# A causal convolution and a ReGLU feed-forward layer on one core: the second unit's convolution in 64x64 matmuls, a shared first Relu, another order of lanes and evictions

## The chip, the cores and the metric

The kernel runs on one core of a Trainium2 chip. The core has a matrix engine (TensorE, PE in the profile, with PEld for its weight loads), VectorE (DVE), ScalarE (ACT), GpSimd (POOL), and SyncE (SP), whose queue here does nothing but issue DMAs. Each engine works through its own list of instructions in order; they wait for each other through semaphores. The metric is the device time of one execution in microseconds.

## The reference

`x` is (8, 4096, 192). A causal convolution of 7 taps, with one set of softmax weights for each of 8 heads of 24 channels, goes into a feed-forward layer with 1536 hidden columns:

```python
w = softmax(weight, axis=-1)                    # (8 heads, 7 taps)
x_pad = concatenate([zeros((B, 6, D)), x], 1)
conv[b, s, h, g] = sum_k w[h, k] * x_pad[b, s + k, h, g]
x = conv.reshape(32768, 192)
out = (maximum(x @ w_gate, 0) * (x @ w_val)) @ w_out
```

Inputs and output are float32; the kernel computes in float16 with float32 accumulation.

## The kernel before

**Units.** The eight sequences are taken as four pairs, `st` = 0 and 1, and each pair is cut into units of 1024 tokens: 16 units. Of each unit the kernel needs `xc`, the convolved tokens turned so that channels lie on partitions: 64 channels of sequence 0 on partitions 0 to 63, the same 64 of sequence 1 on 64 to 127, for 3 groups of channels. Then `gate_val` computes the hidden layer for two windows of 512 tokens, and `project` computes the output for both.

**gate_val.** For each of 12 slices `f` of the hidden layer PE fills two PSUM tiles of 2 x 512 columns, one for the gate and one for the value (`L505`, 12 matmuls each of 64 rows; two of them, for the two sequences, lie in the upper and lower half of the array). ScalarE takes the Relu of the gate tile into `gr` (`L514`), and VectorE multiplies it with the value tile into `hT` (`L515`). There are four PSUM tiles (`psum`, 4 buffers, all named `ps`), so a slice waits for the Relu and the product of the slice two before it.

**project.** Unit 0 uses matmuls over the full array (`half_whole`, `L555`), 48 for each of four half windows; later units use half arrays (`L535`). ScalarE copies the outputs out of PSUM (`L572`) and SP writes them.

**Three ways to convolve.** Unit 0 (groups of tokens 0 and 1) is convolved by PE with x as weights and a band matrix as moving data (`conv_dense`, `L333`), already turned. Units 2 to 15 are convolved by the "lanes" on VectorE, ScalarE and GpSimd, two units ahead: `lane_load` loads, `lane_turn` copies on GpSimd (`L433`) and turns by nine DMA transposes on SP (`L436`), `lane_first` is the first tap on ScalarE (`L469`), `lane_rest` the other taps on VectorE (`L481`, `L454`), and products by ScalarE (`L452`, in `project`) are added on GpSimd (`add`, `L458`).

**The second unit** is what the change rewrites. Its 1024 tokens are cut into sub-blocks of 112 (`SUB`), the last one overlapping, in two groups of five (groups 2 and 3). `load_x` puts the 118 tokens that a sub-block needs on 118 partitions, with both sequences side by side. `conv(g, part)` multiplies by the band of a head (118 x 112) as weights: four heads of a group in each of two calls, one matmul of 240 columns per head (5 sub-blocks, 2 sequences, 24 channels), `L358`. `PLACE` says which bank and slot a head gets. Five copies on ScalarE (`move`, `L373`) put the result into `y` in the order of channels that the turn needs, and five DMA transposes on SP (`L395`) turn `y` straight into `xc[1]`, 112 tokens each.

**Order.** The schedule is by hand (`manual_schedule`): each engine gets its instructions in the order of the Python text. In unit 0: `gate_val(0, 0)`, `lane_turn(2)`, `load_x(3)`, `gate_val(0, 1)`, `conv(2, 0)`, `conv(2, 1)`, `lane_first(2)`, `lane_rest(2)`, then `project`, in which `conv(3, 0)` and `conv(3, 1)` follow the first of four half windows. Unit 1 begins with an `add`, `lane_load(3)` and two more `add` on GpSimd.

The tile pools give a new tile the buffer of an old one of the same name; `epool` has one buffer each for `x_e` and `x_p`, the tiles of `lane_load` and `lane_turn`.

Of the kernel before, what the change touches and what calls it, by code (L numbers as in the profile page):

```python
# [9 lines left out]
F16 = mybir.dt.float16  # L10
# [5 lines left out]
def kernel(  # L16
# [58 lines left out]
    def load_x(g):  # L75


        bp, toks = GROUPS[g]
        xt = xpool.tile([128, GSUB, 2, D], F16, name="x_h")
        rows, step = (SUB, DSUB) if g < 2 else (128, SUB)  # L80
        for st in range(2):
            b = bp + NB * st
            last = toks[-1] - toks[-2] != step
            n_full = len(toks) - int(last)
            src = bass.AP(
                tensor=x.tensor,
                offset=x.offset + (b * S + toks[0] - PAD) * D,
                ap=[[D, rows], [step * D, n_full], [1, D]],
            )
            nc.gpsimd.dma_start(out=xt[0:rows, 0:n_full, st, :], in_=src)  # L90
            if last:
                nc.gpsimd.dma_start(
                    out=xt[0 : SUB + PAD, len(toks) - 1, st, :],
                    in_=x[b, toks[-1] - PAD : toks[-1] + SUB, :],
                )
        return xt

    xts = {}
# [181 lines left out]
    bands = {}  # L280

    def fill_band(a, heads, copy):
        lo, n = heads[0] - HB * a, len(heads)
        part = const.tile([128, n, SUB], F16, name=f"band{heads[0]}")
        for i, h in enumerate(heads):
# [16 lines left out]

    PLACE = {0: (0, 0, 0), 1: (0, 0, 1), 3: (0, 1, 0), 4: (0, 1, 1)}
    PLACE |= {6: (1, 0, 0), 7: (1, 0, 1), 2: (1, 1, 0), 5: (1, 1, 1)}

    def conv_dense(g, c):

# [32 lines left out]
        copy = nc.vector.tensor_copy if c == 1 else nc.scalar.copy  # L342
        copy(out=xc[0][:, c, t0 : t0 + WIN], in_=ps[:, 0, :])

    convs = {}

    def conv(g, part):


        xt = xts[g]  # L350
        bp, toks = GROUPS[g]
        n = len(toks)
        rows = SUB + PAD
        W = 2 * n * G
        ps = psum.tile([128, 2, 512], FP, name="ps")
        for h, (t, bank, slot) in PLACE.items():
            if t == part:
                nc.tensor.matmul(  # L358
                    out=ps[0:SUB, bank, W * slot : W * (slot + 1)],
                    lhsT=band(h),  # L360
                    rhs=xt[0:rows, 0:n, :, G * h : G * (h + 1)],
                    start=True,
                    stop=True,
                    skip_group_check=True,
                )
        if part == 0:
            convs[g] = ypool.tile([128, GSUB, NCH, 2, 64], F16, name="y")
        y = convs[g]

        def move(copy, bank, i0, step_in, c, r0, step_out, width):  # L370
            src = ps[0:SUB, bank, 0 : 2 * W]
            dst = y[0:SUB, 0:n, 0, :, 0:1]
            copy(  # L373
                out=bass.AP(
                    tensor=dst.tensor,
                    offset=dst.offset + 128 * c + r0,
                    ap=[dst.ap[0], [step_out, 2], [NCH * 128, n], [64, 2], [1, width]],
                ),
                in_=bass.AP(
                    tensor=src.tensor,  # L380
                    offset=src.offset + i0,
                    ap=[src.ap[0], [W + step_in, 2], [2 * G, n], [G, 2], [1, width]],
                ),
            )

        if part == 0:
            move(nc.scalar.copy, 0, 0, 0, 0, 0, G, G)
            move(nc.scalar.copy, 1, 0, 0, 1, 8, G, G)
            return
        move(nc.scalar.copy, 0, 0, 0, 2, 16, G, G)  # L390
        move(nc.scalar.copy, 1, 0, 8, 0, 48, 2 * 128 - 48, 16)
        move(nc.scalar.copy, 1, 16, -16, 1, 0, 56, 8)
        for jj, t in enumerate(toks):
            u, k = t // UNIT, min(SUB, UNIT - t % UNIT)
            nc.sync.dma_start_transpose(  # L395
                out=xc[u][:, :, t % UNIT : t % UNIT + k],
                in_=y[0:k, jj].rearrange("p c s r -> p (c s r)"),
            )

    xes, xrs, accs, prods = {}, {}, {}, {}  # L400

# [90 lines left out]
    def gate_val(u, w):  # L492
        h = hpool.tile([128, NFF, 2, WIN], F16, name="hT")
        xcb = xc[u]
        for f in range(NFF):
            if u == 0 and w == 0 and f in (5, 7, 9):
                conv_dense(1, (f - 5) // 2)
            pss = [psum.tile([128, 2, 512], FP, name="ps") for _ in range(2)]
            order = [(i, c) for i in range(2) for c in range(NCH)]
            if u == 0 and w == 0 and f == 0:  # L500
                order = [(i, c) for c in range(NCH) for i in range(2)]
            for i, c in order:
                W = (Wg, Wv)[i]
                for st in range(2):
                    nc.tensor.matmul(  # L505
                        out=pss[i][:, st, :],
                        lhsT=W[64 * st : 64 * st + 64, c, 128 * f : 128 * (f + 1)],
                        rhs=xcb[64 * st : 64 * st + 64, c, WIN * w : WIN * (w + 1)],
                        start=(c == 0),
                        stop=(c == NCH - 1),  # L510
                        tile_position=(64 * st, 0),
                    )
            gr = gpool.tile([128, 2, WIN], F16, name="gr")
            nc.scalar.activation(out=gr[:], in_=pss[0][:], func=ACTF.Relu)  # L514
            nc.vector.tensor_tensor(out=h[:, f], in0=gr[:], in1=pss[1][:], op=ALU.mult)  # L515
        return h

# [75 lines left out]
    def project(u, hs, work):  # L593
        bp, w0 = u * UNIT // S, u * UNIT % S // WIN
        at, done = {}, {}
        order = [(0, 0), (1, 0), (0, 1), (2, 0), (1, 1), (3, 0), (2, 1), (3, 1)]
        if u == 0:
            order = [(i, 2) for i in range(4)]
        if u == NUNIT - 1:
            order = [(0, 0), (1, 0), (0, 1), (2, 0), (1, 1), (2, 3), (3, 0), (2, 4), (3, 1)]  # L600
        for i, turn in order:
            final = u == NUNIT - 1 and i == 3
            h, st = hs[i // 2], i % 2
            if turn in (0, 2):
                at[i] = slots(final)
            if turn in (1, 2):
                for c, k in work[i]:
                    product(nc.scalar, u + 2, c, k)
            if turn > 2:
                n = turn - 3  # L610
                half_pass(h, st, at[i][1], final, 1, done.pop(i, None), (n,))
                put(
                    nc.scalar.copy,
                    nc.sync,
                    at[i][0][0][:, :, D * n : D * n + D],
                    (bp + NB * st) * S + WIN * (w0 + i // 2) + 128 * n,
                    2,
                    256,
                )
                continue  # L620
            if turn == 2:
                half_whole(h, st, at[i][1])
            else:
                done[i] = half_pass(h, st, at[i][1], final, turn, done.get(i))
            if turn:
                evict(at[i][0], (bp + NB * st) * S + WIN * (w0 + i // 2), final, u > 0 and i == 3)
            if u == 0 and i == 0:
                conv(3, 0)
                conv(3, 1)


    for c in range(NCH):
# [9 lines left out]
    for u in range(NUNIT):  # L642
# [2 lines left out]
            add(u + 1, 1)  # L645
        if u == 1:
            lane_load(3)
            add(2, 2)
            add(2, 3)
        hs = []  # L650
# [3 lines left out]
            lane_turn(u + 2)  # L654
        if u == 0:
            xts[3] = load_x(3)
        if 0 < u < NUNIT - 3:
            lane_load(u + 3)
        if lane:
# [5 lines left out]
            add(u + 1, KW - 1)  # L665
        if u == 0:
            xc[1] = xcpool.tile([128, NCH, UNIT], F16, name="xc")
            conv(2, 0)
            conv(2, 1)
        del xc[u]  # L670
        work = [[] for _ in range(4)]
        if u + 2 < NUNIT:
            lane_first(u + 2)
            lane_rest(u + 2)
            todo = [(c, k) for k in (0, 1, 2, 3, 4, 6) for c in range(NCH)]
            todo = [ck for ck in todo if ck not in VECTOR[u > 0]]
            cut = [0, 4, 8, 12, 16] if u == 0 else [0, 5, 10, 15, 16]
            work = [todo[a:b] for a, b in zip(cut, cut[1:])]
# [31 lines left out]
```

## Time and profile before

| what | value |
|---|---|
| runs | 769.03, 769.03, 769.93 us; median 769.03 us |
| the profiled execution, its time | 768.24 us |
| its span, first to last instruction | 766.5 us |
| granted TensorE clock, mean | 1.00 |
| chain of waits, share of the span by engine | PE 98%, DMA 1%, all else under 1% |

The profile is of one execution. Busy times count instructions, not waits; L numbers are lines of the kernel above. A row of the groups of instructions is: line, engine, operation, output and inputs with sizes, count, then busy time in us and the mean of one in ns, then idle time of the engine just before. The convolutions on PE and what belongs to the second unit's are small rows among large ones:

```profile
L505 PE MATMUL ps<-xc,Wv 64*128 64x512 f16 x2304 | 311.8, 376 | 0.2 <-DVE hT L515 0.2
L535 PE MATMUL ps<-Wo,hT 64*128 64x192 f16 x5760 | 240.1, 243 | 0.0
L358 PE MATMUL ps<-x_h,band 118*112 118x240 f16 x16 | 2.0, 268 | 0.0
L358 PEld LDWEIGHTS <-band 118*112 118x112 f16 x16 | 1.6, 129 | 0.4 <-issue 0.4
```

The mean of one PE instruction (376 ns) is longer than the distance between two of them, since they are pipelined: a unit's 288 matmuls of L505 stand 31.08 us in the chain, 0.108 us each. The queue of SP from 20 us on, in order of time:

```profile
30.66 13.19 SPq L436 DMA_TRANSPOSE x_r<-x_p  x9
...
50.93 0.53 SPq L573 DMA_DIRECT2D out_dram<-out_s  x1
51.57 8.51 SPq L395 DMA_TRANSPOSE xc<-y  x5
60.19 1.86 SPq L573 DMA_DIRECT2D out_dram<-out_s  x3
76.30 12.53 SPq L436 DMA_TRANSPOSE x_r<-x_p  x9
```

and GpSimd's, which is idle from 33 us to 60.73 us:

```profile
60.73 3.02 POOL L458 TENSOR_TENSOR prods<-prods 128x1344 f32<-128x1344 f32 x1 [27.56 <-DVE prods L454]
63.71 3.27 POOL L414 DMA_DIRECT2D x_e<-in_x_dram  x4
66.97 6.17 POOL L458 TENSOR_TENSOR prods<-prods 128x1344 f32<-128x1344 f32 x2
73.08 3.19 POOL L433 COPY x_p<-x_e 128x1728 f16<-128x1728 f16 x2
```

### The profile page before, as it was taken

To read this page: it belongs to the slowest core of one execution; us is meant where nothing else is said; L and a number is where in the kernel's file an instruction comes from. 1 tells how busy PE (TensorE), PEld (TensorE's weight loads), DVE (VectorE), ACT (ScalarE), POOL (GpSimd) and SP (SyncE) were. 2 spreads that over 40 slices of the span, in tenths; PEclk is the share of its full clock that TensorE was granted. 3 is DMA by queue.
4 is the path that set the end of the run, shared out by engine and by line. 5 is a ranking of instruction groups with operands and counts; after the bars stand their busy time and mean duration, and the time that the engine had idled before them with its cause. 6 is when DMAs were issued, how large, how long until landed. Compare 5 with 4: busy or idle time off the path is not lost.

```text
span 766.5 us, 24874 instructions
## 1 busy us (share of the span) xinstructions
PE 761.7 (99%) x10842; PEld 502.6 (66%) x10842; DVE 691.8 (90%) x743; ACT 601.1 (78%) x734; POOL 369.8 (48%) x212
## 2 busy tenths in 40 slices
PE   9999999999999999999999999999999999999998
PEld 4495674946749476584765848567494674947648
DVE  6999999999999999999999999999999999996590
ACT  6797887878878787887878878788787887874571
POOL 8608638093470935619166290743908346090000
PEclk9999999999999999999999999999999999999999
DMA  8956727180372804528054271722819131200202
GB/s 121 138 101 114 92 89 89 50 126 6 99 79 64 112 22 93 66 86 94 23 110 48 85 92 44 108 29 85 93 44 114 24 94 38 65 22 18 68 2 84
DMA packets 131826, 56.12 MB, mean 73 GB/s; under 512 B 96757, under 2 KB 131717, under 8 KB 131717
## 3 DMA queue, kind: packets, MB, share of 16 engines
q1 hardware_dynamic: 90805, 38.85, 24.8%
q0 software_dynamic: 40768, 15.59, 18.5%
q8 instruction: 84, 1.38, 0.8%
q14 instruction: 25, 0.20, 0.1%
q10 hardware_dynamic: 144, 0.10, 0.0%
HBM read 31.68 MB, written 25.17 MB: 74 GB/s over the span
## 4 chain that ended last, share of the span: by engine, by line
PE 98%; DMA 1%; DVE 0%; ACT 0%; issue 0%; POOL 0%; POOLq 0%
PE ps L505 65%; PE ps L535 31%; PE ps L555 2%; DMA x_h<-in_x_dram 1%; PE ps L333 0%; PE ps L358 0%; DVE hT L515 0%; ACT gr L514 0%; DVE acc L572 0%; POOL spaced L129 0%; POOLq L694 0%
## 5 line engine op out<-in xcount | busy, mean ns | idle before, releaser
L515 DVE TENSOR_TENSOR hT<-gr,ps 128x1024 f16<-128x1024 f16 x384 | 468.7, 1221 | 37.6 <-ACT gr L514 10.7
L514 ACT ACTIVATE gr<-ps 128x1024 f16<-128x1024 f32 x384 | 392.8, 1023 | 102.8 <-PE ps L505 101.1
L458 POOL TENSOR_TENSOR prods<-prods 128x1344 f32<-128x1344 f32 x70 | 212.4, 3034 | 309.6 <-DVE prods L454 306.2
L505 PE MATMUL ps<-xc,Wv 64*128 64x512 f16 x2304 | 311.8, 376 | 0.2 <-DVE hT L515 0.2
L505 PE MATMUL ps<-xc,Wg 64*128 64x512 f16 x2304 | 311.9, 376 | 0.0
L535 PEld LDWEIGHTS <-hT 64*128 64x128 f16 x5760 | 238.0, 94 | 3.6
L535 PE MATMUL ps<-Wo,hT 64*128 64x192 f16 x5760 | 240.1, 243 | 0.0
L505 PEld LDWEIGHTS <-Wv 64*128 64x128 f16 x2304 | 129.9, 94 | 118.8 <-issue 0.5
L505 PEld LDWEIGHTS <-Wg 64*128 64x128 f16 x2304 | 112.2, 94 | 132.4 <-issue 0.2
L481 DVE SCALAR_TENSOR_TENSOR acc<-x_r,tap,acc 128x576 f32<-128x576 f16 x210 | 154.3, 811 | 1.6 <-DMA x_r<-x_p 1.6
L452 ACT ACTIVATE prods<-x_r,tap 128x448 f32<-128x448 f16 x222 | 130.3, 662 | 0.0
L572 ACT COPY out_s<-ps 128x768 f32<-128x768 f32 (+1 forms) x64 | 46.1, 721 | 54.0 <-PE ps L535 44.0
L414 POOL DMA_DIRECT2D x_e<-in_x_dram x56 | 45.2, 819 | 3.3 <-POOL x_p L433 3.3
L433 POOL COPY x_p<-x_e 128x1728 f16<-128x1728 f16 x28 | 44.7, 1622 | 2.0 <-DMA x_e<-in_x_dram 2.0
L458 POOL TENSOR_TENSOR xc<-prods 128x1344 f16<-128x1344 f32 x14 | 42.4, 3026 | 1.1
L481 DVE SCALAR_TENSOR_TENSOR xc<-x_r,tap,acc 128x576 f16<-128x576 f16 x42 | 31.8, 810 | 0.0
L469 ACT ACTIVATE acc<-x_r,tap 128x576 f32<-128x576 f16 x42 | 29.4, 766 | 0.0
L454 DVE TENSOR_SCALAR prods<-x_r,tap 128x448 f32<-128x448 f16 x72 | 27.3, 445 | 0.0
L572 DVE COPY out_s<-ps 128x384 f32<-128x384 f32 x14 | 7.7, 549 | 14.8 <-ACT out_s L572 14.8
L555 PE MATMUL ps<-Wo,hT 128*128 128x192 f16 x192 | 16.2, 246 | 0.0
L555 PEld LDWEIGHTS <-hT 128*128 128x128 f16 x192 | 15.9, 98 | 0.0
L572 DVE COPY acc<-ps 128x192 f32<-128x192 f32 x1 | 0.4, 357 | 14.2 <-PE ps L535 14.2
(52 smaller groups left out, 63.2 us busy)
## 6 DMA issues: line engine op xcount, KB each, us to landing
out_dram<-out_s SPq DMA_DIRECT2D x62, 384.0 KB
x_e<-in_x_dram POOLq DMA_DIRECT2D x34, 192.0 KB, 6.2
x_e<-in_x_dram POOLq DMA_DIRECT2D x22, 240.0 KB, 4.6
x_r<-x_p SPq DMA_TRANSPOSE x126
Wo<-in_moe_w_out_dram POOLq DMA_DIRECT2D x1, 576.0 KB, 10.2
x_h<-in_x_dram POOLq DMA_DIRECT2D x2, 240.0 KB, 7.8
x_h<-in_x_dram POOLq DMA_DIRECT2D x2, 210.0 KB, 5.2
x_h<-in_x_dram POOLq DMA_DIRECT2D x2, 192.0 KB, 7.5
```

The lines of the kernel that those rows point to most:

```text
L414: nc.gpsimd.dma_start(out=xe[:, j : j + n, st, :, :].rearrange("p j c r -> p j (c r)"), in_=bass.AP(tensor=x.tensor, offset=x.offset + (b ...
L433: nc.gpsimd.tensor_copy(out=xp[:, :, :, st, :], in_=xe[:, :, st, :, :])
L452: engine.activation(out=out, in_=in_, func=ACTF.Copy, scale=scale)
L458: nc.gpsimd.tensor_tensor(out=pr[:, 0] if k < KW - 1 else xc[u][:, :, LDVE:UNIT], in0=pr[:, 0], in1=pr[:, k], op=ALU.add,)
L469: nc.scalar.activation(out=accs[u][:, c, :], in_=shifted(u, c, 0, 0), func=ACTF.Copy, scale=tap[:, c, 0:1],)
L481: nc.vector.scalar_tensor_tensor(out=xc[u][:, c, 0:LDVE] if k == KW - 1 else acc[:, c, :], in0=shifted(u, c, k, 0), scalar=tap[:, c, k : k ...
L505: nc.tensor.matmul(out=pss[i][:, st, :], lhsT=W[64 * st : 64 * st + 64, c, 128 * f : 128 * (f + 1)], rhs=xcb[64 * st : 64 * st + 64, c, WI ...
L514: nc.scalar.activation(out=gr[:], in_=pss[0][:], func=ACTF.Relu)
L515: nc.vector.tensor_tensor(out=h[:, f], in0=gr[:], in1=pss[1][:], op=ALU.mult)
L535: mm = nc.tensor.matmul(out=outs[q], lhsT=h[64 * r : 64 * r + 64, f, st, 128 * q : 128 * (q + 1)], rhs=Wo[64 * r : 64 * r + 64, f, :], sta ...
L555: nc.tensor.matmul(out=outs[q], lhsT=h[:, f, st, 128 * q : 128 * (q + 1)], rhs=Wo[:, f, :], start=(f == 0), stop=(f == NFF - 1),)
L572: one(out=dst[:, step * j : step * j + step], in_=src[:, step * j : step * j + step])
```

## The change

Four edits.

1. **64x64 matmuls.** For groups 2 and 3 `load_x` puts sequence 0 on partitions 0 to 63 and sequence 1 on 64 to 127, and cuts each sub-block into two windows of 64 tokens that give 56 outputs each (`HALF`). `conv` runs, for each head, four matmuls of 120 columns, one for each sequence and window, each in its own quarter of the array (`tile_position`). The weights are the upper left 64 x 64 of the band; for the lower quarters they are read from `lower`, a copy on partitions 64 to 127 that three GpSimd copies make (`fill_lower`, behind `load_x(3)`). The five copies into `y` now cover 128 partitions, and the two sequences come from two PSUM banks.
2. **Gaps closed on GpSimd.** Each window leaves 8 rows that are no output. The five SP transposes of a group now turn all 128 rows of `y` into a tile `turned` (in the buffer of `x_e` for group 2, of `x_p` for group 3), and `close_up` copies 56 of every 64 columns into `xc[1]`: one copy for group 2, two for group 3. `close_up(2)` stands behind `conv(3, 1)`, `close_up(3)` in unit 1 behind `lane_load(3)`.
3. **The first Relu shared.** In the first slice of the first window VectorE takes the Relu of one half of the gate tile (a maximum with 0), ScalarE of the other.
4. **Lanes first.** `conv(2, 0)` and `conv(2, 1)` are called after `lane_first(2)` and `lane_rest(2)`.

```diff
+            n_full = len(toks) - int(toks[-1] - toks[-2] != SUB)
+            for j, n in ((0, n_full), (n_full, len(toks) - n_full)):
+                if n:
+                    nc.gpsimd.dma_start(
+                        out=xt[64 * st : 64 * st + 64, j : j + n].rearrange("p n w d -> p (n w) d"),
+                        in_=bass.AP(
+                            tensor=x.tensor,
+                            offset=x.offset + (b * S + toks[j] - PAD) * D,
+                            ap=[[D, 64], [SUB // 2 * D, 2 * n], [1, D]],
+                        ),
+                    )
...
+    PLACE = [(0, 1, 3, 4), (6, 7, 2, 5)]
+    HALF = SUB // 2
+    lower = const.tile([128, H, 64], F16)
+
+    def fill_lower():
+        for h0, n in ((0, 3), (3, 1), (4, 4)):
+            nc.gpsimd.tensor_copy(out=lower[64:128, h0 : h0 + n], in_=parts[h0][0:64, :, 0:64])
...
-        for h, (t, bank, slot) in PLACE.items():
-            if t == part:
-                nc.tensor.matmul(
-                    out=ps[0:SUB, bank, W * slot : W * (slot + 1)],
-                    lhsT=band(h),
-                    rhs=xt[0:rows, 0:n, :, G * h : G * (h + 1)],
...
+        for slot, h in enumerate(PLACE[part]):
+            for w in range(2):
+                for st in range(2):
+                    nc.tensor.matmul(
+                        out=ps[64 * w : 64 * w + 64, st, W * slot : W * (slot + 1)],
+                        lhsT=lower[64:128, h] if st else band(h)[0:64, 0:64],
+                        rhs=xt[64 * st : 64 * st + 64, 0:n, w, G * h : G * (h + 1)],
...
+                        tile_position=(64 * st, 64 * w),
...
-        for jj, t in enumerate(toks):
-            u, k = t // UNIT, min(SUB, UNIT - t % UNIT)
             nc.sync.dma_start_transpose(
-                out=xc[u][:, :, t % UNIT : t % UNIT + k],
-                in_=y[0:k, jj].rearrange("p c s r -> p (c s r)"),
-            )
+                out=turned[:, :, jj].rearrange("p c w s -> p c (w s)"),
+                in_=y[:, jj].rearrange("p c s r -> p (c s r)"),
+            )
+        turns[g] = turned
+
+    def close_up(g):
+        turned, toks = turns.pop(g), GROUPS[g][1]
+        n = len(toks)
+        n_full = n - int(toks[-1] - toks[-2] != SUB)
+        for j, m in ((0, n_full), (n_full, n - n_full)):
+            t = toks[j % n] % UNIT
+            if m:
+                nc.gpsimd.tensor_copy(
+                    out=xc[1][:, :, t : t + SUB * m].rearrange("p c (n s) -> p c n s", s=HALF),
+                    in_=turned[:, :, j : j + m, :, 0:HALF].rearrange("p c n w s -> p c (n w) s"),
+                )
...
-            nc.scalar.activation(out=gr[:], in_=pss[0][:], func=ACTF.Relu)
+            own = int(u == 0 and w == 0 and f == 0)
+            if own:
+                nc.vector.tensor_scalar(
+                    out=gr[:, 0], in0=pss[0][:, 0], scalar1=0.0, scalar2=None, op0=ALU.max
+                )
+            nc.scalar.activation(out=gr[:, own:2], in_=pss[0][:, own:2], func=ACTF.Relu)
...
                 conv(3, 1)
+                close_up(2)
...
             lane_load(3)
+            close_up(3)
...
             xts[3] = load_x(3)
+            fill_lower()
...
-            conv(2, 0)
-            conv(2, 1)
...
             lane_rest(u + 2)
+            if u == 0:
+                conv(2, 0)
+                conv(2, 1)
```

More of the change, by code (lines that the diff above doesn't have):

```diff
@@ L79, in load_x @@
         xt = xpool.tile([128, GSUB, 2, D], F16, name="x_h")
-        rows, step = (SUB, DSUB) if g < 2 else (128, SUB)
         for st in range(2):
             b = bp + NB * st
[L83 to L88, printed above, removed]
-            )
[L90 to L94, printed above, removed]
-                )
+            if g < 2:
+                src = bass.AP(
+                    tensor=x.tensor,
+                    offset=x.offset + (b * S + toks[0] - PAD) * D,
+                    ap=[[D, SUB], [DSUB * D, GSUB], [1, D]],
+                )
+                nc.gpsimd.dma_start(out=xt[0:SUB, :, st, :], in_=src)
+                continue
+            n_full = len(toks) - int(toks[-1] - toks[-2] != SUB)
[4 more added lines that the diff above has]
+                        in_=bass.AP(
+                            tensor=x.tensor,
+                            offset=x.offset + (b * S + toks[j] - PAD) * D,
+                            ap=[[D, 64], [SUB // 2 * D, 2 * n], [1, D]],
+                        ),
+                    )
         return xt
@@ L279 @@
     nc.scalar.copy(out=xts[0][0:ROWS0, 1:GSUB, 0, :], in_=stage(0, ROWS0, 0, 1, 1, GSUB - 1))
-    bands = {}
+    bands, parts = {}, {}
     def fill_band(a, heads, copy):
@@ L284, in fill_band @@
         part = const.tile([128, n, SUB], F16, name=f"band{heads[0]}")
+        parts[heads[0]] = part
         for i, h in enumerate(heads):
@@ L301 @@
     xc = {}
-    PLACE = {0: (0, 0, 0), 1: (0, 0, 1), 3: (0, 1, 0), 4: (0, 1, 1)}
-    PLACE |= {6: (1, 0, 0), 7: (1, 0, 1), 2: (1, 1, 0), 5: (1, 1, 1)}
+    PLACE = [(0, 1, 3, 4), (6, 7, 2, 5)]
[4 more added lines that the diff above has]
+            nc.gpsimd.tensor_copy(out=lower[64:128, h0 : h0 + n], in_=parts[h0][0:64, :, 0:64])
     def conv_dense(g, c):
@@ L343, in conv_dense @@
         copy(out=xc[0][:, c, t0 : t0 + WIN], in_=ps[:, 0, :])
-    convs = {}
+    convs, turns = {}, {}
     def conv(g, part):
@@ L352, in conv @@
         n = len(toks)
-        rows = SUB + PAD
-        W = 2 * n * G
+        W = n * G
         ps = psum.tile([128, 2, 512], FP, name="ps")
-        for h, (t, bank, slot) in PLACE.items():
-            if t == part:
-                nc.tensor.matmul(
-                    out=ps[0:SUB, bank, W * slot : W * (slot + 1)],
-                    lhsT=band(h),
-                    rhs=xt[0:rows, 0:n, :, G * h : G * (h + 1)],
[L362 to L365, printed above, removed]
+        for slot, h in enumerate(PLACE[part]):
[5 more added lines that the diff above has]
+                        rhs=xt[64 * st : 64 * st + 64, 0:n, w, G * h : G * (h + 1)],
+                        start=True,
+                        stop=True,
+                        tile_position=(64 * st, 64 * w),
+                        skip_group_check=True,
+                    )
         if part == 0:
@@ L368, in conv, with move @@
         y = convs[g]
-        def move(copy, bank, i0, step_in, c, r0, step_out, width):
-            src = ps[0:SUB, bank, 0 : 2 * W]
-            dst = y[0:SUB, 0:n, 0, :, 0:1]
+        def move(copy, pair, i0, step_in, c, r0, step_out, width):
+            src = ps[:, 0, 2 * W * pair : 2 * W * (pair + 1)]
+            dst = y[:, 0:n, 0, :, 0:1]
             copy(
@@ L381, in move @@
                     offset=src.offset + i0,
-                    ap=[src.ap[0], [W + step_in, 2], [2 * G, n], [G, 2], [1, width]],
+                    ap=[src.ap[0], [W + step_in, 2], [G, n], [512, 2], [1, width]],
                 ),
@@ L392, in conv @@
         move(nc.scalar.copy, 1, 16, -16, 1, 0, 56, 8)
-        for jj, t in enumerate(toks):
-            u, k = t // UNIT, min(SUB, UNIT - t % UNIT)
+        turned = epool.tile([128, NCH, GSUB, 2, 64], F16, name=("x_e", "x_p")[g - 2])
+        for jj in range(n):
             nc.sync.dma_start_transpose(
-                out=xc[u][:, :, t % UNIT : t % UNIT + k],
-                in_=y[0:k, jj].rearrange("p c s r -> p (c s r)"),
-            )
+                out=turned[:, :, jj].rearrange("p c w s -> p c (w s)"),
+                in_=y[:, jj].rearrange("p c s r -> p (c s r)"),
+            )
+        turns[g] = turned
[10 more added lines that the diff above has]
+                )
     xes, xrs, accs, prods = {}, {}, {}, {}
```

## The prediction

> **What bounds the kernel now.** I read the page first, then the chain of waits in order of time, then the timeline around the end of unit 0, and last the single instructions whose prices I need. The page's first part:
>
> ```profile
> PE 761.7 (99%) x10842; PEld 502.6 (66%) x10842; DVE 691.8 (90%) x743; ACT 601.1 (78%) x734; POOL 369.8 (48%) x212
> ```
>
> PE is busy 99% of the 766.5 us span, so time can come only from PE's own work or from the few places where PE waits. The chain of work that ended last (start, length, what) shows where these are:
>
> ```profile
> 9.14 1.03 ACT gr L514
> 10.18 0.02 issue
> 10.20 1.23 DVE hT L515
> 11.43 0.04 issue
> 11.47 3.42 PE ps L505 x30
> 14.89 0.56 PE ps L333 x40
> ...
> 41.54 0.99 PE ps L358 x8
> 42.54 3.96 PE ps L555 x48
> 46.50 0.82 PE ps L358 x8
> 47.32 11.88 PE ps L555 x144
> 59.20 31.19 PE ps L505 x288
> ...
> 106.23 31.08 PE ps L505 x288
> ```
>
> The reader is to see three things. After 59.20 us the chain is PE alone, and the change leaves that work as it is. The convolution of the second unit (L358) is 0.99 + 0.82 = 1.81 us of PE time, all that tiling it can ever save. And the chain leaves PE once, at 9.14 us, for the first Relu (ACT) and the first product (DVE): the fifth half-step of the loop needs the PSUM tile that this product frees. So the change has at most about 2 us to win, 0.27% of the time.
>
> The timeline around the end of unit 0 (start, busy time, engine, line, operation):
>
> ```profile
> 41.47 1.06 PE L358 MATMUL ps<-x_h,band 118*112 118x240 f16 x8
> 42.13 2.00 ACT L373 CAST y<-ps 112x480 f16<-112x480 f32 x5 [0.17 <-PE ps L358]
> 43.98 2.15 ACT L469 ACTIVATE acc<-x_r,tap 128x576 f32<-128x576 f16 x3
> 44.15 6.68 SPq L395 DMA_TRANSPOSE xc<-y  x5
> 59.13 0.82 PE L505 MATMUL ps<-xc,Wg 64*128 64x512 f16 x6
> ```
>
> The y evictions start the SP transposes; unit 1 begins only at 59.13 us, so the route from y to xc[1] has room. The instructions of L343 give the price of a 512 column PSUM read on each engine (min/median/max ns):
>
> ```profile
> L343 ACT CAST xc<-ps x3: 585/585/585, 7.1 to 15.5; 128x512 f16<-128x512 f32 x3
> L343 DVE CAST xc<-ps x2: 683/688/692, 7.5 to 19.7; 128x512 f16<-128x512 f32 x2
> ```
>
> **Part 1, the shared Relu.** It replaces one 1.03 us activation by a 512 column VectorE maximum and a 512 column activation. The trace has no VectorE maximum out of PSUM; its bounds are 0.445 us (L454, 448 columns out of SBUF) and 0.81 us (L481, 576 columns, two inputs). I take 0.69 us, the L343 cast of the same shapes. If both halves ran together, gr would be ready at 9.14 + 0.69 = 9.83 instead of 10.17, and the product would end 0.34 us earlier. PE would take all of it: its last matmul before the wait starts at 10.88 and streams 0.21 us, so it stands from 11.10 to 11.47, 0.37 us. But in the built program the ScalarE half waits for no PE value: it waits on VectorE's counter, at the value which that maximum sets. The maximum reads one half of the same PSUM tile and writes one half of the same gr tile, and the order of the two is kept although the halves differ. So they run one after the other: 9.14 + 0.69 + 0.03 + 0.585 = 10.45, against 10.17. That is **+0.28 us**. Behind the waiting activation on ScalarE stands the next Relu (its input is ready at about 10.0, it starts at 10.45 instead of 10.15); the PSUM tile it frees is wanted at about 12.4, so it costs nothing more. Bounds: -0.34 (parallel) to +0.40 (the 0.81 row).
>
> **Part 2, the tiled matmuls.** Sixteen matmuls of 240 columns become 64 of 120 columns on quarters of the array. One of 240 columns takes 0.82 / 8 = 103 ns, so 120 columns stream in 51 ns, and if four go at once a group of 32 streams in 8 x 51 = 0.41 us. That four go at once has one near row: L333, four column tiles, 104 columns. Its forty start at 14.82 and the next L505 matmul starts at 15.39: ten sets in 0.57 us; at 44 ns of streaming each that is 0.44, which leaves 0.13 us for leaving the mode. Entering a mode costs about 0.11 us: 31.19 - 31.08, the first unit after the full-array matmuls against the second. So a group costs 0.11 + 0.41 + 0.13 = 0.65 us.
> Group 3 had 0.82 us with no mode change on either side (L555 uses the full array too): **-0.17 us**. Group 2 is cut short by a wait. Its second half needs the PSUM tile of the product before the last, which VectorE frees at about 41.91 (six products in 7.72 us from 35.48, the sixth ending at 43.20). Before, the fifth matmul started at 41.97, only 0.04 us late. After, the first half is done at about 41.38 + 0.11 + 0.21 = 41.70 and PE stands until 41.97; then 0.21 + 0.13 gives 42.31 against 42.37: **-0.06 us**. Bounds for both groups: no overhead at all and no wait, 1.81 - 0.82 = -1.0 us; or no packing, 64 pairs at the 103 ns of L358, +5.4 us (rival 3). I take the L333 row, as its tiles are the nearest in shape and rate.
> The Trainium skill, "TensorE: Matmul & The Clock Gate", section "Wait — 56ns, not 53.3ns?", says that matmuls never start less than about 25 ns apart, however small they are; that speaks against the change, since 64 x 25 = 1.6 us would leave it nearly nothing. L333 disagrees: forty in 0.57 us are 14 ns apart. By the row part 2 is -0.23 us, by the rule it would be about +0.3 us.
>
> **Part 3, lanes ahead of the y evictions.** On ScalarE three lane activations (43.98 to 45.99, 2.01 us) now precede five y moves (42.13 to 43.98, 1.85 us). Nothing is added, but y is ready 2.01 us later, 45.8 instead of 44.0; queued behind it, the products and out_s copies start where they did. The lanes wait for the first five x_r transposes; the trace's landing events put the fifth at 41.58, before the last Relu of the unit ends at 41.95, so they start at once. DVE's lane work, which began at 44.83, can begin at 43.20; it is off the chain. Who waits for the late y: the second full projection, which reuses that PSUM tile at about 42.3 + 3.96 + 0.65 = 46.9, 1.1 us after it is free. Cost **0**; if the fifth transpose landed 1.5 us later, PE would stand 0.4 us.
>
> **Part 4, turn, then close the gaps.** SP issues the same five transposes per group, after the same queue entries; 128 rows instead of 112 cost what L436's do (1.26 against 1.25 us each). In the trace the last of group 2 lands at 51.98, 7.8 us after its first issue; from 45.85 that is 53.7. One POOL copy of 1680 columns, priced by L433 (1728 in 1.62 us), ends at 55.3; POOL's queue ahead of it is empty (it idles until 60.73). PE asks for it at about 59.1: room 3.8 us, cost **0**. Group 3's copies (1.25 + 0.32 us) stand on POOL behind one add and four load issues, at about 67.0 to 68.6; its columns are first read half a unit after 59.1, at 74.7. They push POOL's adds and the next lane turn, with its nine SP transposes, 1.6 us later; those transposes were issued by 88.83, and the lanes that read them start after 90.4, so they are absorbed. The three `lower` copies (at most 0.4 us each, by L180's 768 columns in 0.82) run at 33 us, 8 us before use. The x loads move the same bytes with as many issues (6 for the two groups); their semaphores were full by 39.7, needed at 41.4 and 46.4.
>
> **Sum:** +0.28 - 0.06 - 0.17 = +0.05 us on this execution's 766.5 us span, 768.24 us with what lies around it. The median of the runs is 769.03, so 769.03 + 0.05 = 769.1 us. About 0.2% (1.5 us) is what a measurement of this kernel can tell from no change.
>
> **Rivals.** (1) *The halves run together*, because the wait is met early: -0.34 - 0.06 - 0.17 = -0.57, 768.5 us. For it: the halves share no data. Against: the built program's wait; and L572, the other place where both engines share a tile, shows ACT at 106.31 for 0.48 us and DVE only from 106.92. (2) *Matmuls pack only in part*. If a pair takes L535's 41 ns (5760 in 15 x 15.84 us, two tiles at a time), a group costs 32 x 41 = 1.32 + 0.24 us: +0.55 for group 2, +0.74 for group 3, +0.28: 770.6 us. Half-way between L333 and L535, at 27 ns, it is 769.7. The rule of the page named above lies in this stretch. (3) *Slower, no packing*: four quarters share one path for weights and load and stream in turn. At 103 ns a pair: 32 x 103 = 3.3 + 0.24 = 3.5 us a group, 2 x 3.5 - 1.81 + 0.28 = +5.5, 774.5 us. It decides from about 40 ns a pair on; L333 at 14 ns speaks against it, but has full rows and quarter columns. (4) *Unit 1 waits for the gap copy*: needs the y route 3.8 us longer than reckoned, then 1 us for each us; 5 us more would give 770.3 us. For it: a serial chain of ACT, SP, DMA and POOL; against: every link has its row.
>
> **How the numbers follow.** Forecast 0.62, rival 1 0.14, rival 2 0.14, rival 3 0.04, rival 4 0.06. The forecast's own range, with single medians 0.5 us apart, is 768.4 to 769.8. The range 768.1 to 770.4 takes in rival 1 and most of rivals 2 and 4. Faster by over 0.2% needs more than rival 1 and the lower bound of part 2 together, -1.3 us: 0.04, for the scatter of a median. Slower: all of rival 3, half of 2, a third of 4: 0.13. Within: 0.83.
>
> **What would show it.** Right: the chain still leaves PE at 9.1 us, now DVE, ACT, DVE, and returns near 11.75; the conv line has 32 matmuls in about 0.65 us in group 3; PE waits a third of a us for VectorE inside group 2; unit 1 starts with no wait on POOL. Wrong: the first Relu's halves overlapping, pairs over 30 ns apart, or PE idle before unit 1.

## The result, and the profile after

The changed kernel takes 770.23 us (median of 22 runs, 769.58 to 772.91). The kernel before, run beside it on the same chip, takes 768.38 us (22 runs, 768.03 to 769.93). The ratio is 1.0024, with a 95% interval of 1.0018 to 1.0031: slower by 1.85 us. The profiled execution of after took 770.21 us with a span of 768.5 us, against 768.24 and 766.5 before, so it shows the same loss: 2.0 us of span.

The page's first part for the kernel after:

```profile
PE 762.1 (99%) x10890; PEld 529.0 (69%) x10890; DVE 692.5 (90%) x744; ACT 600.6 (78%) x734; POOL 378.2 (49%) x218
```

PE's busy time has hardly changed. What has changed is where PE stands. Its longest wait in the trace of after is one that before does not have: 1.40 us, once, for POOL's copy into `xc[1]`, the gap copy of group 2. The timeline of after around it (start, busy time, engine, line, operation, and in brackets the idle time before with its releaser):

```profile
43.87 11.02 DVE L506 SCALAR_TENSOR_TENSOR acc<-x_r,tap,acc 128x576 f32<-128x576 f16 x15
...
54.80 2.27 DVE L506 SCALAR_TENSOR_TENSOR xc<-x_r,tap,acc 128x576 f16<-128x576 f16 x3
55.12 5.93 POOL L420 COPY xc<-x_e 128x1680 f16<-128x1680 f16 x1 [20.94 <-DMA x_e<-y]
...
56.99 2.62 DVE L479 TENSOR_SCALAR prods<-x_r,tap 128x448 f32<-128x448 f16 x7
...
61.10 0.82 PE L530 MATMUL ps<-xc,Wg 64*128 64x512 f16 x6 [1.40 <-POOL xc L420]
```

The copy starts at 55.12 us, while VectorE is in the last taps of unit 2 (L506), and takes 5.93 us. VectorE ends its last product (L479) at 56.99 + 2.62 = 59.61, and the copy ends 1.44 us after that, at 61.05. How long would it take on its own? The two copies of group 3, made by the same line, run while VectorE multiplies out of PSUM. All instructions of L420 (min/median/max ns):

```profile
L420 POOL COPY xc<-x_p x2: 467/909/1351, 67.3 to 68.7; 128x1344 f16<-128x1344 f16 x1, 128x336 f16<-128x336 f16 x1
L420 POOL COPY xc<-x_e x1: 5927/5927/5927, 55.1 to 55.1; 128x1680 f16<-128x1680 f16 x1
```

1344 columns take 1.351 us and 336 take 0.467, which is 0.877 ns a column and 0.172 us to start with. 1680 columns are then 1.65 us, of which the columns alone are 1.47. The last 1.44 us of the long copy are just about its columns: in the 4.49 us before, beside the taps and products, it got almost nowhere.

Where the 2.0 us went can be read from the starts of PE's matmuls. Each row is the time from one start to the next named one, so that a later arrival of the first input does not enter (us):

| stretch | before | after | difference |
|---|---|---|---|
| first matmul of L505 (L530 after) in unit 0 to the last one | 33.32 | 33.75 | +0.43 |
| from there, over group 2's convolution, to the first output matmul (L555, L585 after) | 1.21 | 1.14 | -0.07 |
| from there to the first matmul of group 3's convolution | 3.96 | 4.06 | +0.10 |
| from there to the next output matmul | 0.82 | 0.55 | -0.27 |
| from there to the first matmul of unit 1 | 11.98 | 13.45 | +1.47 |

These make +1.66 us. The first matmul of L530 itself started 0.30 us later in this execution (8.15 against 7.85), which gives 1.97, the later start of unit 1 (61.10 against 59.13) and nearly the whole 2.0 us of span. Of the +0.43, e2 below, whose code is the same in this stretch, shows 33.62, so +0.30 belongs to the shared Relu and 0.13 to this execution. The change itself is then about 1.5 us of the 2.0.

### The profile page after: what moved, and what is told of

It reads as the page before. It is cut to its first block, busy times and chain, and to the rows that moved or that the text cites. A ratio compares the mean times of both kernels' runs of the same rounds, so it can differ in the third digit from the quotient of the medians.

```text
span 768.5 us, 24973 instructions
## 1 busy us (share of the span) xinstructions
PE 762.1 (99%) x10890; PEld 529.0 (69%) x10890; DVE 692.5 (90%) x744; ACT 600.6 (78%) x734; POOL 378.2 (49%) x218
## 4 chain that ended last, share of the span: by engine, by line
PE 92%; POOL 3%; DMA 2%; SPq 2%; issue 1%; ACT 1%; POOLq 0%; DVE 0%
PE ps L530 61%; PE ps L565 31%; SPq L461 1%; POOL xc L420 1%; DMA x_e<-in_x_dram 1%; SPq L407 1%; DMA Wg<-in_moe_w_gate_dram 1%; DMA x_r<-x_p 0%; DMA x_e<-y 0%; POOL Wg L185 0%; POOL x_p L458 0%; POOL Wg L178 0%; POOL Wv L178 0%; ACT acc L494 0%; ACT y L385 0%
## 5 line engine op out<-in xcount | busy, mean ns | idle before, releaser
L544 ACT ACTIVATE gr<-ps 128x1024 f16<-128x1024 f32 (+1 forms) x384 | 392.4, 1022 | 104.9 <-PE ps L530 101.9
L530 PE MATMUL ps<-xc,Wg 64*128 64x512 f16 x2304 | 318.1, 376 | 1.4 <-POOL xc L420 1.4
L530 PE MATMUL ps<-xc,Wv 64*128 64x512 f16 x2304 | 318.0, 376 | 0.4 <-DVE hT L545 0.4
L530 PEld LDWEIGHTS <-Wv 64*128 64x128 f16 x2304 | 138.7, 94 | 110.1 <-issue 0.7
L530 PEld LDWEIGHTS <-Wg 64*128 64x128 f16 x2304 | 130.2, 94 | 116.5 <-issue 2.1
L506 DVE SCALAR_TENSOR_TENSOR acc<-x_r,tap,acc 128x576 f32<-128x576 f16 x210 | 154.3, 811 | 0.0
L506 DVE SCALAR_TENSOR_TENSOR xc<-x_r,tap,acc 128x576 f16<-128x576 f16 x42 | 31.8, 810 | 0.0
L479 DVE TENSOR_SCALAR prods<-x_r,tap 128x448 f32<-128x448 f16 x72 | 27.3, 446 | 0.0
L420 POOL COPY xc<-x_e 128x1680 f16<-128x1680 f16 x1 | 5.9, 5927 | 20.9 <-DMA x_e<-y 20.9
L585 PE MATMUL ps<-Wo,hT 128*128 128x192 f16 x192 | 16.2, 246 | 0.0
L585 PEld LDWEIGHTS <-hT 128*128 128x128 f16 x192 | 15.7, 98 | 0.2
```

What stands on the lines that cost most here:

```text
L506: nc.vector.scalar_tensor_tensor(out=xc[u][:, c, 0:LDVE] if k == KW - 1 else acc[:, c, :], in0=shifted(u, c, k, 0), scalar=tap[:, c, k : k ...
L530: nc.tensor.matmul(out=pss[i][:, st, :], lhsT=W[64 * st : 64 * st + 64, c, 128 * f : 128 * (f + 1)], rhs=xcb[64 * st : 64 * st + 64, c, WI ...
L544: nc.scalar.activation(out=gr[:, own:2], in_=pss[0][:, own:2], func=ACTF.Relu)
L585: nc.tensor.matmul(out=outs[q], lhsT=h[:, f, st, 128 * q : 128 * (q + 1)], rhs=Wo[:, f, :], start=(f == 0), stop=(f == NFF - 1),)
```

## The experiments

Two theories stood for the 5.93 us. **P**: the POOL copy cannot run while VectorE runs its lane work, and has to wait for its end. **S**: it is the shape, a copy with gaps that is slow by itself. A third question was what the other edits are worth when this stall is gone.

**e1, the order of before again.** Edit 4 alone is undone, so that the y moves come first and the gap copy can start earlier, while the lane work comes later.

```diff
             xc[1] = xcpool.tile([128, NCH, UNIT], F16, name="xc")
+            conv(2, 0)
+            conv(2, 1)
...
             lane_rest(u + 2)
-            if u == 0:
-                conv(2, 0)
-                conv(2, 1)
```

> The changed kernel with the lanes behind the y evictions again (edit 4 undone). Theory P (the gap copy on GpSimd gets nothing done while VectorE does its lane work, 18 taps and 7 products): y is ready 2 us earlier and the copy starts near 53 us, but VectorE's lane work then runs from about 45.4 to 61.1 us, so the copy ends about 1.45 us after that, unit 1 starts near 62.6 instead of 61.1: 1.5 us slower than the changed kernel, 771.7 us. Theory S (runs of 56 columns cost GpSimd 3.5 ns a column): the copy takes 5.9 us wherever it stands, 53 to 59, unit 1 starts without a wait: 1.4 us faster than the changed kernel, 768.8 us. The two differ in sign.

Measured: 772.18 us (4 runs), ratio 1.0049 (1.0034 to 1.0065). Its timeline:

```profile
52.71 10.04 POOL L420 COPY xc<-x_e 128x1680 f16<-128x1680 f16 x1 [19.15 <-DMA x_e<-y]
...
58.69 2.62 DVE L479 TENSOR_SCALAR prods<-x_r,tap 128x448 f32<-128x448 f16 x7
```

The same copy with the same bytes now takes 10.04 us. It starts 2.41 us earlier and ends 1.70 us later, at 62.75, and that is again 1.44 us after VectorE's last product (58.69 + 2.62 = 61.31). PE waits 2.9 us. A shape has one price, and here it has two: S falls. What sets the copy's end is the end of the lane work. The SP transposes of group 3 run beside the copy too, but they do not set its end: in e1 the last of them is issued at 58.43 instead of 59.56, earlier, while the copy ends later.

The trace of e1 shows a second cost. When PE goes on after its wait, the granted clock is 0.5 for 3.4 us (62.7 to 66.1), and six matmuls of L530 take 1.28 us instead of 0.65; that makes PE another 1.6 us late. The two executions with a mean granted clock of 0.998, the profiled one among them, took 772.84 and 773.53 us; the two with 1.000 took 771.48 and 771.53, which is what P had, 771.7.

**e2, the gap copy on VectorE.** The copy of group 2 stands among the taps of unit 2 on VectorE itself; `conv(2, ...)` is emitted between `lane_first` and `lane_rest`, which changes no order on ScalarE.

```diff
+            if u == 2 and k == KW - 1:
+                close_up(2, nc.vector.tensor_copy)
...
                 conv(3, 1)
-                close_up(2)
```

> The changed kernel with the gap copy of group 2 on VectorE, between its 15th and 16th tap (group 3 stays on GpSimd). Both theories: PE's wait of 1.4 us at unit 1 goes, 768.8 us. Theory P: the VectorE copy of 1680 columns takes 0.5 to 0.9 us, lane work ends near 60.4, in time for the first product of unit 1 (due at about 61.6). If runs of 56 columns were dear on VectorE too (3 us), the first products of unit 1 would be late by about 1 us and half of the gain lost.

Measured: 768.94 us (10 runs), ratio 1.0006 (0.9997 to 1.0016); span 766.4. The timeline has the copy at a sixth of its time:

```profile
54.77 1.03 DVE L420 COPY xc<-x_e 128x1680 f16<-128x1680 f16 x1 [0.49 <-issue]
```

That is a little above the 0.5 to 0.9 us expected. PE has no wait at the start of unit 1; the last stretch of the table is 11.99 us, that of before. So the stall is the whole loss, as far as the time can tell.

**e3, the Relu whole again.** Edit 3 alone is undone.

```diff
-            nc.scalar.activation(out=gr[:, own:2], in_=pss[0][:, own:2], func=ACTF.Relu)
+            nc.scalar.activation(out=gr[:], in_=pss[0][:], func=ACTF.Relu)
```

> The changed kernel with the first Relu whole on ScalarE again (edit 3 undone). Theory (ScalarE's half waits for VectorE's, in series): PE's wait in the third slice falls by about 0.3 us, VectorE's lane work and with it the end of the gap copy come 0.3 us earlier, the wait at unit 1 stays 1.4 us: 769.9 us. Rival (the halves overlapped and the later start of the profiled run was chance): no change or 0.3 us slower, 770.2 to 770.5 us.

Measured: 770.3 us (9 runs), ratio 1.0028 (1.0015 to 1.004). The first stretch is 33.34 us, as before the change, so the edit's 0.3 us is there; but the time did not move, which I had not expected. The interval is 1.9 us wide and could not have shown 0.3 us; the traces can. The waits of PE in e3:

```profile
PE ps L530 <- POOL xc L420: 1.9, 1, 1.9
```

What PE gained at the start it stood longer here, 1.9 us for 1.4. The chain of waits of after shows what leads up to the copy (start, length, what):

```profile
39.25 3.37 DMA x_r<-x_p
42.62 0.56 ACT acc L494
...
44.69 1.89 ACT y L385 x5
...
51.72 3.12 DMA x_e<-y
...
55.12 5.94 POOL xc L420
```

The end of the copy is again set by the lane work: in e3 the last product ends at 59.23 and the copy at 60.68, 1.45 us later. The lane work begins when ScalarE's lanes have begun, and these hang on the x_r transposes as much as on PE. In after the transposes land at 42.62, just when ScalarE has ended its last Relu of the unit; in e3 ScalarE was ready sooner and its lanes waited 0.87 us for them. While the stall stands, time won or lost by PE in unit 0 is swallowed by it.

**e4 and e8, both undone.** The copy on VectorE as in e2 and the Relu whole as in e3; what stays of the change is the 64x64 matmuls and the lane order. The two runs are the same kernel on two chips.

> Edits 3 undone and the gap copy of group 2 on VectorE: what is left are the tiled matmuls and the lane order. By the predicted terms of these (-0.06 and -0.17 us) 0.2 us under the kernel before: 768.2 us, with no PE wait at unit 1 and the wait in the third slice as before. If the tiled matmuls were worth nothing: 768.4 us.

> The version with edit 3 undone and the gap copy of group 2 on VectorE once more, with more rounds: by the matmul terms 0.23 us faster than before, 768.1 us, 0.03%, which the interval will hardly show; if the tiled matmuls and the copy give nothing, 768.3 us. Neither theory has it slower than 768.6 us.

Measured: 768.25 us (10 runs), ratio 1.0 (0.9991 to 1.0009), and 768.42 us (11 runs), ratio 0.9993 (0.9983 to 1.0002). In the stretches the kernel is ahead by 0.07 + 0.17 us; the comparison resolves about 0.1%, 0.8 us, so it cannot show that.

**e5, spare copies on the kernel before.** It adds work that nobody reads: sixteen POOL copies of 448 plain columns, as soon as group 2's columns have landed. It takes the price of a POOL copy beside taps, products and multiplications without the change.

```diff
                 conv(3, 1)
+                spare_copy = epool.tile([128, 16, 448], F16, name="x_e")
+                for i in range(16):
+                    nc.gpsimd.tensor_copy(out=spare_copy[:, i], in_=xc[1][:, i % NCH, 0:448])
```

> The kernel before, with 16 spare GpSimd copies of 448 columns (contiguous, f16, about 0.57 us each when free) behind the turn of group 2; nothing reads what they write, so the time should stay near 768.3 us. They become ready near 52 us, while VectorE does its lane work until 60.6 us. Theory P (GpSimd is held up by VectorE's taps, which read two tensors from SBUF, and by its products): the first copy is hardly done before 60 us, and the rest follow at about 0.57 us each from 60.6 us on. If only the taps hold it: the copies run from 58 us on. If only the products hold it: four or more are done by 58 us. If neither (the copy's shape was the cause): all 16 are done by 61.5 us.

The instructions of the new line (min/median/max ns, first and last start):

```profile
L632 POOL COPY x_e<-xc x16: 560/561/9328, 53.3 to 69.6; 128x448 f16<-128x448 f16 x16
```

and VectorE's products beside it:

```profile
59.57 2.62 DVE L454 TENSOR_SCALAR prods<-x_r,tap 128x448 f32<-128x448 f16 x7
```

The first copy takes 9.33 us, from 53.28 to 62.61, and ends 0.42 us after VectorE's last product (its seven products run from 59.57 for 2.62 us, to 62.19). The other fifteen run beside VectorE's multiplications and take 0.56 us each. A plain copy of 448 columns is held like the one with gaps, so this is neither the shape nor anything else of the change; and it is held through the taps and through the products alike.

That the time would stay was a miss: one run gave 776.01 us. The copies delay POOL's queue by 9.4 us (its first add starts at 70.12 instead of 60.73; 1.6 us of that are the later start of unit 1 in this execution, which the copies did not cause). Behind them are the load and the lane turn of unit 3; the taps of unit 3 begin on VectorE at 96.48 instead of 91.98, and the chain of waits runs from the spare copies over the x_e load, the lane turn, the taps and an out_s copy to PE at 114.8, which stood 0.9 us there. Another 2.3 us it stands at 98 us in the output projection:

```profile
PE ps L535 <- SPq L548: 2.3, 1, 2.3
```

L548 is a marker in SP's queue between two turns of the projection (`nc.sync.nop`; so this queue does not only issue DMAs). It stands behind the nine transposes of unit 3, which the spare copies delayed too: the last of them ends at 98.14 us instead of 88.83. As PE goes on, the granted clock is 0.5 for 3.4 us (98.6 to 102.0). By the starts of PE's matmuls this makes up the 6.8 us by which the span is longer: 1.6 before unit 1, 2.5 at the marker, 1.7 by the clock behind it, and 1.0 at 114.8. POOL is busy 48% of the span in the kernel before and is not on its chain, and still its queue has no 9 us to spare there.

**e6, the shared Relu alone**, on the kernel before.

```diff
-            nc.scalar.activation(out=gr[:], in_=pss[0][:], func=ACTF.Relu)
+            own = int(u == 0 and w == 0 and f == 0)
+            if own:
+                nc.vector.tensor_scalar(
+                    out=gr[:, 0], in0=pss[0][:, 0], scalar1=0.0, scalar2=None, op0=ALU.max
+                )
+            nc.scalar.activation(out=gr[:, own:2], in_=pss[0][:, own:2], func=ACTF.Relu)
```

> The kernel before with edit 3 alone (first Relu shared). Theory (in series): from the start of VectorE's maximum to the first product 1.35 us against 1.06 us from the start of the Relu before, PE waits 0.3 us longer in the third slice, and nothing hides it: 768.6 us, 0.3 us slower, which is within what the comparison can tell (0.04%). Rival (the halves overlap): 0.7 us between, 768.0 us.

Measured: 768.63 us (10 runs), ratio 1.0 (0.9991 to 1.0009). The first stretch is 33.64 us against 33.32: +0.32, in the trace and below what the time shows. In the trace of after the same step looks like this:

```profile
9.61 0.69 DVE L541 TENSOR_SCALAR gr<-ps 128x512 f16<-128x512 f32 x1 [0.26 <-PE ps L530]
...
10.34 2.53 ACT L544 ACTIVATE gr<-ps 128x512 f16<-128x512 f32 x3 [1.21 <-DVE gr L541]
...
10.97 3.48 DVE L545 TENSOR_TENSOR hT<-gr,ps 128x1024 f16<-128x1024 f16 x3 [0.66 <-ACT gr L544]
```

ScalarE's half starts at 10.34, when VectorE's has ended, and its releaser is that half. From the first Relu to the product it is 10.97 - 9.61 = 1.36 us, where before had 10.20 - 9.14 = 1.06.

**e7, the lane order alone**: e4 with `conv(2, ...)` ahead of the lanes, as in e1. Of the change only the 64x64 matmuls and the gaps are left.

> Tiled matmuls, the gap copy of group 2 on VectorE, the first Relu whole and the lanes behind the y evictions (edits 3 and 4 undone). If the lane order is worth nothing, as the prediction had it: 768.2 us, like the run with the lanes first. If it is what gives VectorE room for the copy: VectorE's lane work begins about 2 us later, ends near 62 us, the first product of unit 1 is 1.1 us late and PE waits about 1 us in the third slice of unit 1: 769.3 us.

Measured: 768.33 us (10 runs), ratio 0.9996 (0.9986 to 1.0005). VectorE's lane work ends 0.66 us later than in e2 (61.18 against 60.52), and PE waits 0.2 us for a product early in unit 1. By the starts of its matmuls it loses 0.4 us there: from the first matmul of unit 1 to the end of the span e7 has 707.76 us, e4 and e8 have 707.36. I had expected about 1 us: a miss. With the copy off POOL the lane order is worth 0.4 us in the trace, and nothing that the times can show.

**e9, the two halves in two PSUM tiles.** e8, with the shared Relu again, but the two sequences of the first gate tile in two PSUM tiles, and in the first slice the value matmuls of channel group 0 ahead of the gate's.

```diff
-            pss = [psum.tile([128, 2, 512], FP, name="ps") for _ in range(2)]
+            pss = [psum.tile([128, 2, 512], FP, name="ps") for _ in range(3 if first else 2)]
...
-                order = [(i, c) for c in range(NCH) for i in range(2)]
+                order = [(1, 0), (0, 0), (0, 1), (1, 1), (0, 2), (1, 2)]
...
-                        out=pss[i][:, st, :],
+                        out=pss[2][:, 0, :] if first and i == 0 and st == 0 else pss[i][:, st, :],
...
-                    out=gr[:, 0], in0=pss[0][:, 0], scalar1=0.0, scalar2=None, op0=ALU.max
+                    out=gr[:, 0], in0=pss[2][:, 0], scalar1=0.0, scalar2=None, op0=ALU.max
```

> The version of e8 with the first gate's two sequences in two PSUM tiles, so that nothing is shared and the halves of the first Relu can overlap (in the first slice the value matmuls of channel group 0 go first, as the third tile comes free later). Theory (only the shared PSUM tile put the halves in series): from the start of VectorE's maximum to the first product 0.72 us instead of 1.35, PE's wait in the third slice goes (-0.37 us), up to 0.2 us of it given back by the later third tile: 0.2 to 0.4 us faster than e8, 0.4 to 0.6 us under the kernel before. Rival (the series is not from the tile): 1.35 us between, as in the changed kernel, 0.3 us slower than e8.

```profile
9.11 0.69 DVE L544 TENSOR_SCALAR gr<-ps 128x512 f16<-128x512 f32 x1 [0.16 <-PE ps L533]
...
9.28 0.60 ACT L547 ACTIVATE gr<-ps 128x512 f16<-128x512 f32 x1 [0.69 <-PE ps L533]
...
9.94 1.22 DVE L548 TENSOR_TENSOR hT<-gr,ps 128x1024 f16<-128x1024 f16 x1
```

Now each half waits for PE alone, they overlap, and the product starts 0.83 us after the first half instead of 1.36. The first stretch is 33.06 us, 0.26 less than before. The time: 768.45 us (12 runs), ratio 0.9999 (0.999 to 1.0009). By the stretches this version should be ahead of before by 0.26 + 0.24 = 0.5 us; the runs do not confirm a gain, and no version tried beats the kernel before by more than the comparison can tell.

## Why the prediction was right or wrong

The forecast was no change, 769.1 us; the kernel became slower by 0.24%, and what happened is the fourth rival, which had a chance of 0.06. That 770.23 us lies inside the stated range of 768.1 to 770.4 is luck: the forecast's own range ended at 769.8, the upper end was drawn for rivals 2 and 4, and the base under it was 0.65 us too high. Of the signs that were named, "PE idle before unit 1" came, which was to mean wrong. Step by step:

- **The shared Relu, +0.28 us**: measured +0.30 to +0.32 (e2, e6). The mechanism, two halves in series because they share a tile, is the one in the trace, and e9 shows that it is the PSUM tile: with two of them the halves overlap. But the term does not simply add: while PE stands at unit 1 it is hidden (e3).
- **The 64x64 matmuls, -0.06 and -0.17 us**: measured -0.07, and -0.27 + 0.10 = -0.17. Four go at once: sets of four follow each other every 52 ns, 13 ns a matmul, as the L333 row said. Between the two halves of group 2 there is a gap of 0.30 us (42.40 to 42.70), where a wait of 0.27 for VectorE's product was reckoned. The upper bound, +5.4 us without packing, is not what its figures give: 64 x 0.103 - 1.81 is 4.8, and 5.3 with the four mode changes; nothing else hung on it.
- **Lanes first, cost 0**: right for PE itself. The lanes began as soon as ScalarE was free, though only just: in e3, e4 and e9 they waited 0.87, 0.36 and 0.65 us for the x_r transposes. And the projection that reuses y's PSUM tile did not wait for the late y. Unforeseen was that the edit helps the new copy: it brings the end of VectorE's lane work forward, and without it (e1) the stall is 1.5 us longer. With the copy elsewhere the edit is worth 0.4 us in the trace (e7).
- **The gap copy, cost 0**: the step that failed. "One POOL copy of 1680 columns, priced by L433 (1728 in 1.62 us), ends at 55.3 ... room 3.8 us". The route up to the copy was nearly as reckoned. Against the moment when PE asks (61.10 - 1.40 = 59.70 in after), the turned columns landed 0.53 us later than forecast and the copy began another 0.29 us later, behind three semaphore steps on POOL. The copy then took 5.93 us instead of 1.62. Together 0.53 + 0.29 + 4.31 = 5.13 us more than reckoned; less the room of 3.8 that is 1.33, and with 0.05 us from the copy's end to PE's start it is the 1.4 us of the wait. Rival 4 looked for the delay in the y route; only 0.82 of the 5.13 us lie on the way to the copy, the rest in the copy itself.

The failure is in the choice of the row. L433's copies run where VectorE multiplies with one input in PSUM; the gap copy runs where VectorE does its lane work out of SBUF. The trace of before never has both at once: of its 129 POOL copies, adds and memsets none overlaps one of VectorE's 324 taps and products. Its timeline around the lane work of unit 3:

```profile
91.98 11.02 DVE L481 SCALAR_TENSOR_TENSOR acc<-x_r,tap,acc 128x576 f32<-128x576 f16 x15
...
107.17 3.03 POOL L458 TENSOR_TENSOR prods<-prods 128x1344 f32<-128x1344 f32 x1 [17.07 <-DVE prods L454]
```

POOL idles 17 us, through all of this lane work, and starts when the products are done (105.10 + 1.90 = 107.00). "POOL's queue ahead of it is empty" was true, and the reason for it should have been asked. So the copy's price was one that the trace did not show, and it was given a single value with no upper bound. The bound was to be had from the prediction's own figures: the lane work ends at 60.59 in before and was to come 44.83 - 43.20 = 1.63 us forward, to 58.96; a copy that must wait for it and then takes 1.62 us ends at 60.6, 1.5 us after PE asks at 59.1. That is close to the stall that was measured, 1.47. The words against rival 4, "every link has its row", were wrong for this link.

The base also moved: 769.03 was a median of 3 runs, and 22 runs give 768.38. Added to the measured terms (+0.30 - 0.07 - 0.17 + 1.47 = +1.53) that is 769.9 us, against 770.23. The measured ratio, 1.0018 to 1.0031, is 1.4 to 2.4 us, so the 1.53 lies within it.

## What to carry to other kernels

Price a GpSimd instruction by a row in which VectorE does the same work beside it, and if the profile has no such row, bound it by the end of VectorE's work plus its own time. Room on a serial route is counted against every engine that its links share something with, not only against their queues. And a change of a few tenths of a microsecond on a 768 us kernel is settled by intervals between the starts of its matmuls, since the medians of ten runs cannot see it.

## What the runs showed of the hardware

A POOL copy made next to no progress while VectorE ran chains of taps (two SBUF inputs, 576 columns every 0.73 us) and of products (448 columns every 0.363 us): 5.93, 10.04 and 9.33 us for copies that take 0.56 us (448 columns, measured) and 1.65 us (1680 columns, worked out above) beside VectorE's multiplications out of PSUM. In all three the rest after VectorE's last product, 1.44, 1.44 and 0.42 us, is about what the columns alone need at 0.877 ns (1.47, 1.47 and 0.39); e3's copy, 5.37 us with a rest of 1.45, is a fourth. VectorE for its part was not slowed: its first fifteen taps took 11.02 us in after, where POOL is idle through all of them, and 11.03 in e1, where the copy stands beside the last five.

The Trainium skill, "SBUF — State Buffer", section "🔬 SBUF: two separate sides", says that VectorE and GpSimd share one pair of ports as an exclusive lock, held for a whole instruction by a VectorE operation with two SBUF inputs or in a two-port mode, and that the other engine is then blocked entirely. The runs agree, and the prediction would have been another had it been weighed. They go further in one point: over a chain of VectorE instructions, whose records follow each other without a gap (0.81 us long, 0.73 us apart), the pair did not pass to POOL between one and the next, in up to 8.9 us of waiting (e5, 53.28 to 62.19). Which of the two conditions the products meet, with one input from SBUF, the runs do not tell.

In both traces in which PE waited for more than 2 us in the middle of its work, e1 (2.9 us) and e5 (2.3 us), the granted clock was 0.5 for the 3.4 us after the wait, which cost another 1.6 to 1.7 us; in after and e3, with waits of 1.4 and 1.9 us, it stayed at 1.0 there. A mean granted clock of 0.998 stands in 2 of 22 executions of after, 2 of 4 of e1, 2 of 9 of e3 and the one of e5, and in none of the versions without such a wait (63 executions) nor of the kernel before (68 with a clock on record). No run here tests what brings it on, but a wait of PE can cost more than its own length.
